# A gated linear attention with an MLP behind it: the input loads get turns of their own, and GpSimd makes the constants

## The chip, the cores and the metric

The kernel runs on one core of a Trainium2 chip. The metric is the time of one execution on the device, in microseconds (us). For the kernel before, the median of three runs is 440.69 us (437.28 to 443.71). The profile below comes from one more execution, which took 438.34 us; the span from its first to its last instruction is 436.6 us. The engines are named as the profile names them: PE (TensorE matmuls), PEld (its weight loads), DVE (VectorE), ACT (ScalarE), POOL (GpSimd), SP (SyncE, which here does nothing but start DMA transfers, in the order of the program). The granted TensorE clock was 1.00 of full speed.

## The reference, cut to what matters

```python
# q, k, v, alpha: (B=4, H=8, S=768, D=48), float32
for t in range(S):
    state = alpha[:, :, t, :, None] * state + einsum('bhd,bhe->bhde', k[:, :, t], v[:, :, t])
    y[:, :, t] = einsum('bhd,bhde->bhe', q[:, :, t], state)
x = y.transpose(0, 2, 1, 3).reshape(B, S, H * D)          # 4 x 768 x 384
xn = (x - mean(x)) / sqrt(var(x) + 1e-6) * g_ln
out = x + maximum(xn @ w_ch1, 0) @ w_ch2                  # 384 -> 1536 -> 384
```

The two weight matrices arrive as 64-bit floats and are rounded to 32 bits on the chip.

## The kernel before, in words

**Tiling.** The sequence is cut into six chunks of 128 tokens. One *step* of attention is one chunk of one batch, so there are 6 x 4 = 24 steps, lettered a to x: a to d are the four batches of chunk 0, e to h those of chunk 1, and so on. A step goes through these stages, each on the line given:

- `la` = Ln(alpha) on ACT (L277); cumulative sums of it as a matmul with the triangle `tri` (`lps`, L283 in chunk 0, L287 in later chunks); Exp of these with both signs on ACT (L290, L291); k and q times those on DVE (`qk`, L293 and L295).
- eight PE transposes with the identity `ident` (`tps`, L320), copied out by ACT and DVE (L325, L327); the scores (`aps`, L336 in chunk 0, L344 later), put under a mask by DVE (`at`, L349 or L354); k times v (`ups`, L370); the state update (L379 on DVE, later L383 on DVE and L385 on POOL) with a `gate` that goes out to DRAM as a row and comes back as columns (two small DMAs, L300 and L360); and the output (`yps`, L396 or L406).
- the layer norm (L413 to L439) and three transposes into `xT` (`xps` on PE, L445, then L448 on DVE or L452 on ACT).

The MLP of chunk 0 multiplies plainly: a *hidden turn* (L475, letters Y for batches 0 and 1, Z for 2 and 3) makes one of 12 column blocks for two batches, and L487 projects back. The chunks after it use a scheme with fewer products (hidden products L764, second products L587) and more additions on DVE and POOL.

**Weights.** They come in 12 pieces of 768 KB (L191). Each is rounded by five DVE instructions (L203 to L213) and one on ACT (L209) before PE may use it. Column blocks 0 and 1 of the hidden layer need piece 0, blocks 2 and 3 piece 1, and so on.

**Order.** Nothing is scheduled at run time. Each stage is a Python generator that records its instructions up to its next `yield`. The string `ORDER` has one letter per `next()`: a letter lets its generator record one more part. So `ORDER` alone fixes the order in which each engine's queue is filled, and SP's queue too. Every engine works through its queue in order and waits on semaphores.

**Loads.** They have no letters in the kernel before. The four loads of alpha for chunk 0 stand ahead of everything. k, q and v of chunk 0 are issued by the attention steps of batches 0 and 2. Alpha, k and q of chunks 1 and 2 are issued together at one fixed place in the steps of batches 1 and 3 of the chunk before (the call `load(c + 1, b // 2, "akq")`), a pair of batches per transfer (384 KB each). From chunk 3 on, `load_one` does the same a batch at a time (192 KB each) into buffers that were claimed once. `v`, and a copy `vx` with its half chunks crossed, are issued behind the output of a step. Alpha, k and q share six buffers (`tag="in"`), so a new load waits for the last read of the tile that lay in its buffer. SP waits in its queue for that, and whatever is queued behind waits too. In the built program every transfer also waits for the one that was issued eight before it, since there are eight completion semaphores.

**Constants.** `tri`, `ident` and a triangle for half chunks lie side by side in one tile `consts` of 128 x 320. The host puts them into the program, and ACT's queue loads them (160 KB) at the start.

Of the kernel before, what the change touches and what calls it, by code (L numbers as in the profile page):

```python
# [9 lines left out]
FP32 = mybir.dt.float32  # L10
# [4 lines left out]
AOP = mybir.AluOpType  # L15
# [7 lines left out]


ORDER = (
    "aaaabbddcccaacbababbaaaadbbbbaaaccdfbbbbcaeeeafcadbbbcecAfedgAccdddeeeeedghffcAc"
    "caabbbdddffffcccfbAgggihbheceeejeeeifaagggggedddjhhchaagdfffBcfiijeejjbbaafkhecc"
    "cffiBjhhjehjjjggYYcciiiBBYYiihddgghhldddChffffhhfYCffYYYddkhiiklCkjhjileegigegjk"
    "jjlCZZZZZZAlDgCFhfgeDZBhYZFZYhhllhhhYlYOiEgjDDFklkEkkilZOgZgggnYmkYYYmEEillllmjj"
    "llZimmnnknkkiYYZZimoZZGiGYYnnnnYYSSHYHSSmGemmmZZZepHZYnFIGnZZOZlIkkkHkomlojJSgJm"  # L30
    "mIJjjKkkkkIQQiSZkLQSjQmmmmmipSniPPPKOKSLLWppooWPWWWhfggnhhfXXiXSSSiXXXPPjjXXPooo"
    "WQiQpQQXpimkkXXOOlnnWmkkmMMnnWmmmlMMMSSSlMMoSMMrrSooWMMMrMMMMMPRqMMMMRnkkMMMoMjr"
    "lRpMMMppMnlnpoooonqqlppppppqqWMMMMqMMMMMMMMMMMMoOolljmMMnnMMMJqsMMOWMpMlMMMqqMRR"
    "RRRMMRMMMMlqsqqrrttqoNNooRRppqqNNppnssMWMRMMqMMMNNNNMMjNsNNsMMMMqMWMMNpNMjMMMMNM"
    "tttNNMMMMurrrrMMMMMrqXqXXXMMMMXXnOntsXXXssoXMsqqMMMMMMMMMMMMMXnMMMRMMMMMMtMMrrtt"
    "qqMMMrrrvMvttuutssssssrttuOMMOOMMMMrvvMMMMmMtpptMMMMMMMpMMMMMtMMRRRRRsRRsttsMrrs"
    "LssmvvmMMMMMrRNNMMpNNppMMMMMRrRonovsosMvMssoMMNNvNNNMvMMtMMuuwMNssRNMMMNNuuuuMMM"
    "MMMrrxMMNMMNqrtNMMMMoMxvvvvoXOwuuuunXXXXXMtttXMMMMMMXXXXuOMMMMtMMMxxxtMMMMMMMMRM"
    "OqOwMMMMwwMMMMMMMMvvtMMMRMMMMMtqMMRMRRRMuMMqqMMMMMwwwwwMMMMxxMMMMMMMxxwwwRxRRNNu"
    "uvwvvxMxxxxwMMRRMMMMvwNNNNNNMuRMMMMNxxxwwwwwMMMMMMwrrNNNMuMwwNMMMMXrXXXXXMMNNNMM"  # L40
    "MMMuMMMMMXXMMMMvMMMwXXxxXMMMMMMMOOvvMMMMMxMuvuMMMRMMMMMMMMMRRRuMMMMMMMxMMMKMMMMM"
    "MMMMMMxxxRRMMMMRMMMMRRxMMMNNNRuwMMMMNRMMMvvuXXXXXXXXXOMMMNNNMMMMVVVVXXVVVNVMVVNN"
    "OMVVVVMMMVVVVRNNVVVMMMMNMVVNVVVVMMNVVVVVVVVVVRRVVVVVRRMMMVMMVVVRRRMMMVVMMVONVVVO"
    "VRMMVRVVVRNNVVMNMNMMMMMRNOMMMMNMMMNONMMMMMVRNNNMMMNNMMMMMMMMMNMNMMNMMMMMMMMM"
)


# [1 line left out]
def kernel(  # L49
# [51 lines left out]
    raw = ctx.enter_context(tc.tile_pool(name="raw", bufs=B // 2))  # L101
# [7 lines left out]

    HS = P // 2  # L110
    halves = [slice(HS * s, HS * s + HS) for s in range(2)]
    r = np.arange(P)
    const_np = np.concatenate([np.triu(np.ones((P, P), np.float32)), np.eye(P, dtype=np.float32),
                               np.tile(np.triu(np.ones((HS, HS), np.float32)), (2, 1))], 1)

    raws = {}

    def load(c, m, names):

        bs = range(2 * m, 2 * m + 2)  # L120
        rows = slice(c * P, (c + 1) * P)
        for n, src in (("a", alpha), ("k", k), ("q", q)):
            if n in names:
                t = raw.tile([P, 2, 2, NP, D], FP32, name=f"r{n}", tag="in", bufs=6)
                step = 1 if n == "a" and c == 0 else 2
                for i in range(0, 2, step):
                    nc.sync.dma_start(
                        t[:, i:i + step].rearrange("t b i p d -> t b (i p d)"),
                        src[bs.start + i:bs.start + i + step, rows].rearrange("b t h d -> t b (h d)"))
                raws.update({(n, c, b): t[:, b - bs.start] for b in bs})  # L130
        if "v" in names:
            vn = raw.tile([P, 2, 2, NP, D], FP32, name="vn", tag="vn")
            nc.sync.dma_start(vn.rearrange("t b i p d -> t b (i p d)"),
                              v[bs.start:bs.stop, rows].rearrange("b t h d -> t b (h d)"))
            vx = None
            if c:


                vx = raw.tile([P, 2, NP, D], FP32, name="vx", tag="vx")
                src = v[bs.start:bs.stop, rows].rearrange(  # L140
                    "b (s t) (i p) d -> s i t b (p d)", s=2, i=2)
                for h in range(2):
                    nc.sync.dma_start(vx[halves[h]].rearrange("t b p d -> t b (p d)"),
                                      src[1 - h, 1 - h])
            for b in bs:
                raws["v", c, b] = vn[:, b - bs.start], vx[:, b - bs.start] if c else None

    lone = {}

    def load_one(n):  # L150

        c, b = divmod(n, B)
        for n, src in (("a", alpha), ("k", k), ("q", q)):
            if n not in lone:
                lone[n] = raw.tile([P, 2, 2, NP, D], FP32, name=f"r{n}", tag="in", bufs=6)
            t = raws[n, c, b] = lone[n][:, b % 2]
            rows = src[b, c * P:(c + 1) * P]
            nc.sync.dma_start(t.rearrange("t i p d -> t (i p d)"),
                              rows.rearrange("t h d -> t (h d)"))
# [5 lines left out]
    for m in range(B // 2):  # L165
        load(0, m, "a")

    w1 = cpool.tile([P, NJ // 2, NF, 2 * P], FP32, name="w1")
    w2 = cpool.tile([P, NJ, DM], FP32, name="w2")
# [79 lines left out]
    def eq_of(c, b):  # L249
        return eqs[b if c < 2 else b % 2]  # L250
# [13 lines left out]
    def attention(c, b):  # L264


        whole, last = c == 0, c + 1 == NCB
        if whole and b % 2 == 0:
            load(0, b // 2, "kq")
            yield  # L270
            load(0, b // 2, "v")
            yield

        qk = qk_of(c, b).rearrange("t n p i c -> t n i p c")[:, :, :, :, :D]
        eq = eq_of(c, b).rearrange("t p i c -> t i p c")[:, :, :, :D]
# [5 lines left out]
        a = las.pop((c, b))  # L281
# [28 lines left out]
        yield  # L310
        at = ats[b % len(ats)]
        if not whole:
# [46 lines left out]
        with nc.allow_non_contiguous_dma(reason="two rows to columns"):  # L359
            nc.sync.dma_start(gate[:, :ne], row[:ne].rearrange("o (p r) -> r o p", p=NP))  # L360
        yield
        vn, vx = raws["v", c, b]
# [29 lines left out]
        for p in range(NP):  # L392
            for i in range(2):
                for s in range(2):
                    if whole:
                        nc.tensor.matmul(yps[0][halves[s], i, p], at[:, p, i, s], vn[:, i, p],  # L396
                                         start=True, stop=True)
                        continue
                    for r in range(2):
                        if r == i:  # L400
                            rs = slice(64 * i, 64 * i + D)
                            of, by = qT[rs, p, s], (now, mid)[s][rs, p]
                        else:
                            of, by = at[halves[r], p, s], (vn[halves[r], i, p] if s == r else
                                                           vx[halves[r], p])
# [436 lines left out]
    turns |= {chr(ord("A") + i): take_weights(i) for i in range(len(pieces))}  # L842
    turns |= {"M": mlp(), "V": hidden_products(NCB - 1), "S": combine_first(), "W": combine_weights(), "R": relus(),
# [34 lines left out]
```

## Time and profile before

| | before |
|---|---|
| median of three runs (lowest, highest) | 440.69 us (437.28, 443.71) |
| the profiled execution | 438.34 us |
| its span | 436.6 us |
| PE busy | 426.7 us, 98% |
| DVE busy | 339.8 us, 78% |
| ACT busy | 201.6 us, 46% |
| POOL busy | 149.7 us, 34% |
| moved by DMA | 45.53 MB, mean 104 GB/s |
| DMA in 0 to 10, 10 to 20, 20 to 30 us | 271, 284, 275 GB/s |

The shares are means over a span whose parts differ. [...] In the last row the DMA engines move between two and three times the mean of the span.

### The profile page before, as it was taken

Reading aid. Unit: us, or ns where it says so; the run is one execution under the profiler, and the core shown is the slowest. Engines: PE = TensorE matmul, PEld = TensorE weight load, DVE = VectorE, ACT = ScalarE, POOL = GpSimd, SP = SyncE. Lnnn points to the kernel's source line nnn. Section 1 sums busy time; section 2 is a strip of 40 time slices with the busy share of each in tenths; the row PEclk is TensorE's granted clock in tenths of the full one; section 3 lists DMA queues with packets and bytes.
Section 4 is the critical chain, followed back from the end, with each engine's and each line's share of the span. In section 5 each row is a group of like instructions: output and inputs, shape, how many; then the busy total and the mean of one; then the engine's idle time right before and its main releaser. Section 6 shows DMA issues by size and latency. Waiting matters only on the chain.

```text
span 436.6 us, 11599 instructions
## 1 busy us (share of the span) xinstructions
PE 426.7 (98%) x4760; PEld 380.9 (87%) x4760; DVE 339.8 (78%) x654; ACT 201.6 (46%) x499; POOL 149.7 (34%) x164
## 2 busy tenths in 40 slices
PE   7988999999999999999999999999999999999996
PEld 5877888876668889999889999889998899999996
DVE  3976989999989788986767758666886589956874
ACT  4687777662325665223277643454505643041100
POOL 1002110111002753051854050872043670756514
PEclk9999999999999999999999999999999999999999
DMA  8988799755035451316214035100014000001201
GB/s 281 289 239 230 202 293 305 186 165 165 2 114 142 98 178 41 108 38 136 67 38 148 18 74 165 1 2 4 20 56 144 2 1 2 0 20 54 72 8 67
DMA packets 54973, 45.53 MB, mean 104 GB/s; under 512 B 26204, under 2 KB 51036, under 8 KB 54920
## 3 DMA queue, kind: packets, MB, share of 16 engines
q1 hardware_dynamic: 54376, 44.63, 34.9%
q8 instruction: 37, 0.61, 0.6%
q10 hardware_dynamic: 544, 0.17, 0.2%
q14 instruction: 16, 0.13, 0.1%
HBM read 35.25 MB, written 9.53 MB: 103 GB/s over the span
## 4 chain that ended last, share of the span: by engine, by line
PE 85%; DVE 5%; DMA 5%; ACT 1%; SPq 0%; issue 0%; DVEq 0%
PE hps L764 30%; PE ops L587 29%; PE ops L487 7%; PE hps L475 4%; PE yps L406 4%; PE tps L320 3%; DMA ws<-in_moe_w_ch_dram 3%; PE aps L344 3%; DMA ra<-in_alpha_dram 2%; PE xps L445 2%; PE ups L370 2%; PE lps L287 1%; DVE w L205 1%; DVE at L354 1%; DVE w L213 0%; PE yps L396 0%
## 5 line engine op out<-in xcount | busy, mean ns | idle before, releaser
L603 POOL TENSOR_TENSOR ob<-ob,u 128x192 f32<-128x192 f32 x40 | 26.9, 683 | 66.8 <-DVE ob L600 56.4
L764 PE MATMUL hps<-sum,w 128*128 128x256 f32 x192 | 47.7, 379 | 0.0
L385 POOL TENSOR_TENSOR mid<-mid,gate 112x192 f32<-112x192 f32 x20 | 10.8, 548 | 98.7 <-DMA gate<-row 48.5
L587 PE MATMUL ops<-w,hT 128*128 128x192 f32 x224 | 40.1, 327 | 0.0
L764 PEld LDWEIGHTS hps<-sum,w 128*128 128x128 f32 x192 | 35.9, 190 | 4.5
L815 ACT ACTIVATE hT<-hT 128x512 f32<-128x512 f32 x48 | 28.3, 625 | 23.7 <-POOL hT L786 15.7
L587 PEld LDWEIGHTS ops<-w,hT 128*128 128x128 f32 x224 | 36.8, 190 | 0.4
L764 PE MATMUL hps<-xT,w 128*128 128x256 f32 x136 | 34.7, 380 | 0.0
L475 PE MATMUL hps<-xT,w 128*128 128x256 f32 x144 | 33.6, 383 | 0.5 <-ACT xn L429 0.5
L487 PE MATMUL ops<-w,hT 128*128 128x384 f32 x96 | 32.0, 488 | 0.0
L475 PEld LDWEIGHTS hps<-xT,w 128*128 128x128 f32 x144 | 26.4, 190 | 4.2 <-ACT xn L429 0.6
L327 ACT COPY qT<-tps 112x512 f32<-112x512 f32 x24 | 13.8, 579 | 35.3 <-PE tps L320 35.2
L597 DVE TENSOR_TENSOR ob<-ops,ob 128x192 f32<-128x192 f32 x50 | 17.3, 352 | 16.4 <-PE ops L587 7.1
L587 PE MATMUL ops<-ws,sum 128*128 128x192 f32 x160 | 28.5, 326 | 0.0
L487 PEld LDWEIGHTS ops<-w,hT 128*128 128x128 f32 x96 | 17.8, 190 | 11.5 <-ACT x L413 0.2
L764 PEld LDWEIGHTS hps<-xT,w 128*128 128x128 f32 x136 | 25.2, 190 | 3.0
L320 PE MATMUL tps<-consts,qk 128*112 128x128 f32 x176 | 24.7, 275 | 2.6 <-DVE qk L295 2.5
L587 PEld LDWEIGHTS ops<-ws,sum 128*128 128x128 f32 x160 | 26.4, 190 | 0.1
L320 PEld LDWEIGHTS tps<-consts,qk 128*112 128x112 f32 x176 | 20.0, 133 | 6.4 <-DVE qk L295 3.4
L587 PE MATMUL ops<-ws,hT 128*128 128x192 f32 x128 | 23.5, 327 | 0.4 <-DVE hT L574 0.4
L344 PE MATMUL aps<-qT,kT 48*64 48x64 f32 x640 | 23.7, 221 | 0.0
L783 POOL TENSOR_TENSOR hT<-hT,u 128x512 f32<-128x512 f32 x8 | 10.3, 1287 | 37.0 <-DVE u L782 37.0
(230 smaller groups left out, 1171.7 us busy)
## 6 DMA issues: line engine op xcount, KB each, us to landing
ws<-in_moe_w_ch_dram SPq DMA_DIRECT2D x12, 768.0 KB
vn<-in_v_dram SPq DMA_DIRECT2D x12, 384.0 KB
kept<-x SPq DMA_DIRECT2D x24, 192.0 KB
ob<-kept SPq DMA_DIRECT2D x24, 192.0 KB
out_dram<-ob SPq DMA_DIRECT2D x19, 192.0 KB
ra<-in_alpha_dram SPq DMA_DIRECT2D x16, 192.0 KB
rk<-in_k_dram SPq DMA_DIRECT2D x6, 384.0 KB
rq<-in_q_dram SPq DMA_DIRECT2D x6, 384.0 KB
```

The lines of the kernel that those rows point to most:

```text
L320: nc.tensor.transpose(tps[:, p], qk_of(c, b)[:, i, p].rearrange("p a b -> p (a b)")[:, :R], ident)
L327: nc.scalar.copy(out=qT, in_=tv)
L344: nc.tensor.matmul(aps[0][halves[1 - i], p, s], kT[rs, p, s], qT[rs, p, s], start=True, stop=True)
L385: nc.gpsimd.tensor_mul(new, new, by)
L406: nc.tensor.matmul(yps[r][halves[s], i, p], of, by, start=True, stop=True)
L475: nc.tensor.matmul(hps, w1[:, j // 2, f, j % 2 * P:][:, :P], xT_of[0][:, f, bs], start=(f == 0), stop=(f == NF - 1))
L487: nc.tensor.matmul(ops_of[b], hT_of[c][:, j, b], w2[:, j], start=(j == 0), stop=(j == NJ - 1))
L587: nc.tensor.matmul(acc, lhs[:, j], rhs[:, j], start=(j == 0), stop=(j == NT - 1))
L597: nc.vector.tensor_add(x, acc, x)
L603: getattr(nc.gpsimd, f"tensor_{op}")(x, x, y)
L764: nc.tensor.matmul(acc[:, i], w, b, start=True, stop=True)
L815: nc.scalar.activation(out=x, in_=x, func=AFT.Relu)
```

## The change

Three things change; the arithmetic on PE, DVE and ACT has the same instructions in the same numbers (2,512 matmul instructions, 636 on DVE).

First, the loads of alpha, k, q and v become four generators with the letters 0 to 3, so that each single transfer has a place of its own in `ORDER`. Chunk 0 is loaded a batch at a time for k and q too, which makes four transfers more (229 on SP against 225). From chunk 3 on, the buffers stay as they were.

Second, `consts` is made by seven GpSimd instructions, and its DMA goes away.

Third, `ORDER` is another string, 1,546 letters for 1,516. It orders all work anew, not only the loads.

```diff
 ORDER = (
-    "aaaabbddcccaacbababbaaaadbbbbaaaccdfbbbbcaeeeafcadbbbcecAfedgAccdddeeeeedghffcAc"
...
+    "00aa00b1cda1a2b22bcc11103abbccdaaa2abbbbdcc2caabbbcffeeedda0bbAabfffaadaeef1dddf"
+    "hfc3dfbghAbddfgaaacbac2dddbhAghcccadbefebhge3ehhh0hggjfggfA3fbhajhBcccgecee2dfff"
...
-    def load(c, m, names):
...
-    def load_one(n):
...
+    def loads(n):
+        src = {"a": alpha, "k": k, "q": q}[n]
+        lone = None
+        for c in range(NCB):
+            for m in range(B // 2):
+                if c < 3:
+                    t = raw.tile([P, 2, 2, NP, D], FP32, name=f"r{n}", tag="in", bufs=6)
+                elif lone is None:
+                    t = lone = raw.tile([P, 2, 2, NP, D], FP32, name=f"r{n}", tag="in", bufs=6)
+                step = 2 if 0 < c < 3 else 1
                 for i in range(0, 2, step):
+                    bs = slice(2 * m + i, 2 * m + i + step)
                     nc.sync.dma_start(
                         t[:, i:i + step].rearrange("t b i p d -> t b (i p d)"),
+                        src[bs, c * P:(c + 1) * P].rearrange("b t h d -> t b (h d)"))
+                    raws.update({(n, c, 2 * m + j): t[:, j] for j in range(i, i + step)})
+                    yield
+
+    def loads_of_v():
+        for c in range(NCB):
+            for m in range(B // 2):
...
+                nc.sync.dma_start(vn.rearrange("t b i p d -> t b (i p d)"),
+                                  v[bs, rows].rearrange("b t h d -> t b (h d)"))
+                raws.update({("v", c, 2 * m + i): vn[:, i] for i in range(2)})
+                yield
+                if c:
...
+                    for h in range(2):
+                        nc.sync.dma_start(vx[halves[h]].rearrange("t b p d -> t b (p d)"),
+                                          src[1 - h, 1 - h])
...
+                    yield
 
     consts = cpool.tile([P, 2 * P + HS], FP32, name="consts")
-    nc.scalar.dma_start(consts, nc.inline_tensor(const_np, name="consts").ap())
...
+    nc.gpsimd.memset(tri, 1.0)
+    nc.gpsimd.affine_select(out=tri, in_=tri, compare_op=AOP.is_ge, fill=0.0, base=0,
+                            pattern=[[1, P]], channel_multiplier=-1)
+    nc.gpsimd.memset(ident, 0.0)
+    nc.gpsimd.affine_select(out=ident, in_=ident, compare_op=AOP.not_equal, fill=1.0, base=0,
+                            pattern=[[-1, P]], channel_multiplier=1)
+    nc.gpsimd.memset(consts[:, 2 * P:], 1.0)
+    for h in halves:
+        part = consts[h, 2 * P:]
+        nc.gpsimd.affine_select(out=part, in_=part, compare_op=AOP.is_ge, fill=0.0, base=0,
+                                pattern=[[1, HS]], channel_multiplier=-1)
...
-        if whole and b % 2 == 0:
-            load(0, b // 2, "kq")
-            yield
-            load(0, b // 2, "v")
-            yield
...
-        n = c * B + b + 2
-        if c < 2 and b % 2:
-            load(c + 1, b // 2, "akq")
-        elif n == 3 * B + 1:
-            load_one(n - 1)
-            load_one(n)
-        elif 3 * B + 1 < n < NCB * B:
-            load_one(n)
-        yield
...
-        if not last and b % 2:
-            load(c + 1, b // 2, "v")
-        yield
...
+    turns |= {"012"[i]: loads("akq"[i]) for i in range(3)} | {"3": loads_of_v()}
```

In the new order the first transfers on SP are alpha of the four batches, then k and q of batch 0 and 1, each batch by itself. The first weight piece stands in both orders behind the same 5.12 MB of transfers (itself counted). The second stands behind 8.49 MB instead of 10.46 MB, the third behind 10.47 MB instead of 12.25 MB, the fourth behind 11.25 MB instead of 14.03 MB. The second pair of v of chunk 0 stands behind 5.92 MB instead of 3.15 MB, alpha for batches 2 and 3 of chunk 1 behind 4.34 MB instead of 5.52 MB, and alpha for the first pair of chunk 2 behind 7.50 MB in both. The last 45 matmul instructions and what follows them are the same products in the same order.

On POOL the new queue begins with two memsets of 128 x 128, then the setting that POOL makes before its first arithmetic instruction (a MODIFY_POOL_CONFIG in the trace; before, it stands at the first L385), the selects for `tri` and `ident`, a memset, the memset of the first `at`, the selects for the half triangles, and the memset of the second `at`.

More of the change, by code (lines that the diff above doesn't have):

```diff
@@ new lines @@
+    "fJPekKKhhehhQnooSSSeehLfOikkkggieggnnL22SiQjgL33nnjpgq00WWPP3SXXrXSjkXpPkniSSWnX"
+    "nnoWOSXnnWkPOkknXQiQmQpmSSSippnkmllnnnplpl3ppmnXMPXXWmMMMWMMjMMMOOOSMXMMmmmMMMMM"
+    "QMMmooMMMMoMMMroppqoooooRkRnppp1o13WqpMq2qkkMMMooMMMjMMMM3WM3MMWMMMnn0tMMMpRRMMR"
+    "MMMMRMqqqMMM1MssqWqqqRrr1pRpoqpppMLMM0RMNNssNNWMMMMRRRMMNNNNNjj2lollOOMMrMNMM2MN"
+    "NuqqooMM3WMMsl2MMMM2rlmmrMMMjMNNNNMsMMMMMMMMMssqrrMMXjXXsMMMuXX1rrtsqqXXXXqttqqq"
+    "tMMMMMXX0MMMMMMMMMMM0wMMMMqqMMvtMMttstMMMMr0rrvstpusttttRRsvMMuMMM11sMrMpMMMM2pM"
@@ L45 @@
+    "MVVVVVVVVVNNNNNNNVVVVVVVVMMXMVVVMMMMMNNMNNNNVVVMMVVVVVVMVVOMMMMVVVVVVVVVVVMRMMVV"
+    "NNVVNVMMMVVMVRVRRVVVVVKRMMOVVVVMOMRRRRMMMNRMMRRMNNMMMNNNMMMMOMMMMMNNMMMNNNNMMMMJ"
+    "OMMMNMMNMNMMMNMMMMMMMMMMMM"
 )
@@ L111 @@
     halves = [slice(HS * s, HS * s + HS) for s in range(2)]
-    r = np.arange(P)
-    const_np = np.concatenate([np.triu(np.ones((P, P), np.float32)), np.eye(P, dtype=np.float32),
-                               np.tile(np.triu(np.ones((HS, HS), np.float32)), (2, 1))], 1)
     raws = {}
-    def load(c, m, names):
[L120 to L125, printed above, removed]
+    def loads(n):
[8 more added lines that the diff above has]
+                step = 2 if 0 < c < 3 else 1
@@ L126, in load @@
                 for i in range(0, 2, step):
+                    bs = slice(2 * m + i, 2 * m + i + step)
                     nc.sync.dma_start(
                         t[:, i:i + step].rearrange("t b i p d -> t b (i p d)"),
[L129 to L146, printed above, removed]
@@ L148 @@
-    lone = {}
-    def load_one(n):
[L152 to L159, printed above, removed]
+                        src[bs, c * P:(c + 1) * P].rearrange("b t h d -> t b (h d)"))
@@ new lines, in loads @@
+                    raws.update({(n, c, 2 * m + j): t[:, j] for j in range(i, i + step)})
[3 more added lines that the diff above has]
+            for m in range(B // 2):
+                bs, rows = slice(2 * m, 2 * m + 2), slice(c * P, (c + 1) * P)
+                vn = raw.tile([P, 2, 2, NP, D], FP32, name="vn", tag="vn")
+                nc.sync.dma_start(vn.rearrange("t b i p d -> t b (i p d)"),
[3 more added lines that the diff above has]
+                if c:
+                    vx = raw.tile([P, 2, NP, D], FP32, name="vx", tag="vx")
+                    src = v[bs, rows].rearrange("b (s t) (i p) d -> s i t b (p d)", s=2, i=2)
+                    for h in range(2):
+                        nc.sync.dma_start(vx[halves[h]].rearrange("t b p d -> t b (p d)"),
+                                          src[1 - h, 1 - h])
+                    raws.update({("x", c, 2 * m + i): vx[:, i] for i in range(2)})
+                    yield
@@ L361, in attention @@
         yield
-        vn, vx = raws["v", c, b]
+        vn = raws["v", c, b]
         heads = [slice(0, 64), slice(64, R)]
@@ L404, in attention @@
                             of, by = at[halves[r], p, s], (vn[halves[r], i, p] if s == r else
[L405 removed]
+                                                           raws["x", c, b][halves[r], p])
                         nc.tensor.matmul(yps[r][halves[s], i, p], of, by, start=True, stop=True)
```

29 lines of the change are left out of this document (9 added, 20 removed).

## The prediction

> **What bounds the kernel now.** I read the page first (busy shares, then the slices over time), next what PE waited for, then the rows of the start and the DMA rates by stretch, and last the chain.
>
> ```profile
> span 436.6 us, 11599 instructions
> ...
> PE 426.7 (98%) x4760; PEld 380.9 (87%) x4760; DVE 339.8 (78%) x654; ACT 201.6 (46%) x499; POOL 149.7 (34%) x164
> ...
> PE   7988999999999999999999999999999999999996
> ...
> DMA  8988799755035451316214035100014000001201
> ```
>
> PE is the bound. It has room only in the first six or so slices (10.9 us each) and in the last. The DMA engines are busy in just those first slices and mostly idle later. So there are two stages: a front of about 65 us with PE short of work, and a rest in which PE never stands.
>
> ```profile
> PE tps L320 <- DVE qk L295: 2.5, 2, 1.4
> PE lps L287 <- ACT la L277: 1.9, 2, 1.3
> ```
>
> These two (in total, times, longest) are most of PE's waits. Both have a load behind them:
>
> ```profile
> 8.32 0.56 DVE L293 TENSOR_TENSOR qk<-rk,lps 128x384 f32<-128x384 f32 x1 [5.65 <-DMA rk<-in_k_dram]
> 9.24 0.56 DVE L295 TENSOR_TENSOR qk<-rq,eq 128x384 f32<-128x384 f32 x1 [0.36 <-DMA rq<-in_q_dram]
> ...
> 9.86 2.02 PE L320 MATMUL tps<-consts,qk 128*112 128x128 f32 x16 [1.18 <-DVE qk L295]
> ...
> 29.45 0.52 ACT L277 ACTIVATE la<-ra 128x384 f32<-128x384 f32 x1 [1.62 <-DMA ra<-in_alpha_dram]
> ```
>
> PE's first transposes (9.86) wait for DVE, and DVE for k and q; at 29.45 alpha of chunk 2 is late. The DMA engines were full meanwhile (columns after the busy times: clock, DMA share, GB/s):
>
> ```profile
> 0.00:10.00 10.00, 7.78 (x25) 5.68 (x26) 3.14 (x14) 4.81 (x9) 2.04 (x6) 1.00 0.84 271
> 10.00:20.00 10.00, 9.47 (x162) 7.94 (x162) 8.86 (x18) 5.39 (x13) 0.00 (x0) 1.00 0.94 284
> 20.00:30.00 10.00, 8.69 (x177) 7.45 (x175) 9.60 (x17) 8.21 (x22) 0.95 (x1) 1.00 0.92 275
> 30.00:40.00 10.00, 9.78 (x250) 9.03 (x251) 6.76 (x17) 9.44 (x29) 1.91 (x3) 1.00 0.74 181
> ```
>
> The chain says the same, and shows SP at 34.88 held up by a buffer, with a weight piece behind it:
>
> ```profile
> 24.80 4.62 DMA ra<-in_alpha_dram
> ...
> 34.88 0.37 SPq L127
> 35.30 1.25 SPq L360
> 36.60 6.36 DMA ws<-in_moe_w_ch_dram
> ...
> 405.98 27.32 PE ops L587 x168
> ```
>
> **PE's lateness.** Busy time hides the losses of the front, so I count otherwise: the work ordered ahead of an instruction on PE, at the pace of the trace, taken from its start. The paces are from starts to starts, long stops left out: eight transposes 0.93 us, scores of a step of chunk 0 1.0, of a later step with its `lps` 1.05, `yps` 1.0, `ups` 0.3 (0.6 later), `xps` 0.34, a hidden turn 1.34, the warm-up 3.6, `lps` of chunk 0 2.6 for all four. The first hidden turn (L475) has 30.1 us ahead and starts at 39.09: 9.0 late. The fifth has 37.1 ahead and starts at 48.31: 11.2 late. The last has 78.5 ahead and starts at 89.7: still 11.2. After that only 0.4 us is lost (244.7), and 3.3 us pass behind the last matmul. So 11.2 us of the 436.6 are lost in the front. What the change does to that number is what it does to the time.
>
> **The change, part by part.**
>
> *Work.* Same matmuls, DVE and ACT instructions: 0. Four transfers more cost SP 4 x 0.4 = 1.6 us of issuing (L127, 0.37 to 0.43 each). SP idles for tens of us later, and in the front the DMA backlog hides it; without that cover it is 1.6 us at most. The tail is the same products in the same order: 3.3 us stay.
>
> *Order of the loads.* To fit the late alpha: 7.50 MB stand up to it on SP, 0.16 of `consts` beside them; at 277 GB/s (mean of the first three stretches) 27.7 us, and it was used at 29.45, so 1.8 more. With that fit each load gives a lateness: the arrival less the PE work ahead of its user.
> - Before: alpha of chunk 2 arrives at 29.45, 21.6 ahead: 7.9 late. The second weight piece landed at 42.98 and was rounded by 48.17 (5.2 us of DVE), 37.1 ahead: 11.1 late. That is the 11.2.
> - After, alpha of chunk 2: 27.1 + 1.8 = 28.9, now with 26.4 ahead: 2.5.
> - After, second pair of v in chunk 0 (moved back): 5.92 MB, 21.4 + 1.8 = 23.2, its `ups` has 18.8 ahead: 4.4. This is the latest load.
> - After, second weight piece: 8.49 MB, 30.6 + 1.8 + 5.2 = 37.6, 37.1 ahead: 0.5. Third: 37.8 + 7.0 = 44.8, 44.3 ahead: 0.5.
> With 4.4 in the place of 11.1, what is late next is DVE.
>
> *DVE in the front.* From the first mask copy (L349, at 13.05) to the second `xT` (L448, done at 38.9) it had 21.7 us of work in 25.9. In the new order 18.3 us stand between the same two. A start near 13.0 gives 31.3 plus waits of 1.5 (the gates and v as above) to 4.2 (as before): 32.8 to 35.5 for the first hidden turn, with 29.1 ahead. Lateness 3.7 to 6.4.
>
> *Constants on POOL.* No select and no setting of POOL with nothing else to wait for is in the trace. A select costs between 0.1 (memset 128x1) and 1.3 us (POOL on 128x512, L783, 1,287 ns); I take 0.5, the nearest in size (L385, 112x192, 548 ns). For the setting there is this row (durations, first and last start):
>
> ```profile
> L385 POOLq MODIFY_POOL_CONFIG  x2: 9/9/9, 28.1 to 28.2; - x2
> ```
>
> POOL's next event is at 33.12, 5.0 us on, but the profile lays this wait to a gate's DMA. So the setting costs 0 to 5.0; I take 5.0, since nothing shows that POOL could have begun earlier. Two memsets from 0.73 (0.17 each, as DVE's L227): `tri` is ready at 1.1 + 5.0 + 0.5 = 6.6, where before PE had it by 4.5. Then `lps` 0.65, the two Exp 0.8, k and q on DVE 1.0: first transposes at 9.1 to 9.3, not 9.86, as k and q of batch 0 alone stand behind 1.38 MB, not 1.57 + 0.16 (0.35 / 0.277 = 1.3 us sooner, 7.9). At a cost of 0, k and q decide, and transposes begin at 8.6 or so. Both are under the old time; `ident` (7.1) and the `at` memsets (8.2 and 10.1) are ready before their users (9.2 and 12). If this cover went, each us of POOL would be a us of PE's start.
> [...]
>
> *The middle.* Behind 100 us of PE work, loads in the new order have 5.4 us or more between the point of PE's work where SP can issue them and the use; before, the shortest were 6.5 and 7.2 and no wait came of them. I cost this at 0, hidden behind PE; if one load of 192 KB met a full queue it would be 1 to 2 us.
>
> *Sum.* Lateness by loads 4.4, by DVE 3.7 to 6.4; the two mix, so 6.0, against 11.2: 5.2 us gained. 438.34 - 5.2 = 433.1 for an execution like the profiled one. The runs' median lies 2.35 above it, so I forecast **435.5** as a median. The runs spread over 6.4 us, and 2% (8.8 us) is about what a measurement of this kernel can tell from no change.
>
> **Rivals.**
> 1. *The gain is made in the front and lost again in the middle.* For: the new order is another one throughout, and its tightest round trips from PE over ACT or DVE and back have only 0.4 to 0.6 us to spare at some six places. Against: the order before has such places too (0.5 us), with a single wait of 0.4 us after 68 us. Five such waits of 1 us each take it all: 440.5.
> 2. *SP runs dry (slower).* Loads of 192 KB fill the eight places with 1.6 MB at most, 5.7 us at 277 GB/s; with pairs 2.4 to 3.1 MB. SP in the new order stands at `row` and `gate` transfers at about 9 to 14 us, with a weight piece and the second v behind them. Each us of empty DMA engines puts that v a us later. From 11.2 - 4.4 = 6.8 us of emptiness on, the kernel is slower than before. For it: in 30 to 40 us the rate fell to 181 GB/s while SP was held up for 2.3 us. Against: by 10.4 us 3.9 MB can be issued, work for 14 us. At twice that emptiness, 13.6: 440.69 + 6.8 = 447.5.
> [...]
> 4. *Much better than this:* v and DVE are no bound, and only the start remains, 3.0 us (9.2 less 6.2 ahead): 8.2 gained, 432.5.
>
> **How the numbers follow.** Forecast 0.55, rival 1 0.20, rival 2 0.10, rival 3 0.07, rival 4 0.08. Range 430 to 442: the low end is rival 4 with the runs' scatter, the high end rival 1 with it; rival 2 is left out. Faster by over 2% (under 431.9) needs rival 4 and a good run: 0.10. Slower by over 2% (over 449.5) is the worse part of rival 2 and unseen waits: 0.08. Within 2%: 0.82.
>
> **What would show it.** First transposes at 8.6 to 9.4 (POOL's part; over 10 speaks for rival 3), the setting of POOL at about 1.1 and its first select at most 5 us later; the first hidden turn at 33 to 36, not 39.09; no wait of DVE's L203 for the second piece; PE without waits of over 0.5 us from 50 us on; the last matmul 3.3 us ahead of the end. A DMA rate under 240 GB/s in 10 to 30 us, or PE waits in the middle that add up to 3 us, would make me wrong.

## The result, and the profile after

The changed kernel takes **436.76 us** as a median (433.0 to 440.07, 20 runs), the kernel before 439.41 us in the same series (436.96 to 443.71, 20 runs). The ratio is 0.9937 with a 95% interval of 0.991 to 0.9965: faster by 0.6%, a small gain that is really there. The profiled execution took 435.69 us with a span of 433.9, against 438.34 and 436.6 before. So some 2.7 us came, where the forecast counted 5.2 for an execution like that one.

The page of the changed kernel, in the order in which the page of the kernel before was read (span, busy time by engine, then the busy tenths of PE and of the DMA engines in 40 slices of 10.8 us):

```profile
span 433.9 us, 11625 instructions
...
PE 425.5 (98%) x4760; PEld 380.3 (88%) x4760; DVE 336.1 (77%) x654; ACT 202.6 (47%) x499; POOL 149.8 (35%) x171
...
PE   8999998999999999999999999999999999999996
...
DMA  8877869675435614314233024022012100001201
```

PE is the bound as before. The front of PE is a little fuller, but its seventh slice (65 to 76 us) has an 8 where the kernel before had a 9. What PE waited for (total, times, longest), by the view of waits:

```profile
PE hps L458 <- DVE ws L211: 1.6, 1, 1.6
...
PE tps L306 <- DVE qk L290: 0.9, 2, 0.8
PE lps L282 <- ACT qT L313: 0.8, 1, 0.8
```

The two large entries of before (2.5 at the transposes, 1.9 at `lps`) are down to 0.9 and 0.8. A new one of 1.6 us stands in front of a hidden turn. The chain of waits in the first 75 us shows both (start, duration, what):

```profile
18.85 5.80 DMA vn<-in_v_dram
24.69 0.61 PE ups L356 x13
...
26.53 6.32 DMA ra<-in_alpha_dram
32.87 0.52 ACT la L272
...
33.92 0.75 PE lps L282 x3
...
37.04 2.79 PE hps L458 x12
...
69.64 0.82 issue
70.46 4.58 PE hps L458 x20
```

The second pair of `v` is issued at 18.85 and used at 24.69; alpha of chunk 2 is issued at 26.53 and used at 32.87; the hidden turns begin some 4 us of PE's program behind it. By the count of the prediction (start on PE less the PE work ordered ahead):

| point | before | forecast after | after |
|---|---|---|---|
| first transposes | 9.86 us | 9.1 to 9.3 | 9.31 |
| `ups` with the second `v` pair, late by | | 4.4 | 5.9 |
| `lps` of chunk 2 with its alpha, late by | 8.4 | 2.5 | 7.5 |
| first hidden turn, start / late by | 39.09 / 9.0 | 32.8 to 35.5 / 6.0 | 36.97 / 7.9 |
| at 100 us, late by | 11.1 | 6.0 | 9.1 |
| last PE instruction starts | 432.95 | | 430.35 |

The forecast counted the alpha from its arrival, not from the start of `lps`; so counted, it is 7.9 before and 6.5 after (used at 32.87, 26.4 ahead) where 2.5 was forecast. Of the 11.1 us, 2.0 are gone by 100 us, and the later part loses 0.6 less than before (2.6 in all at the last PE instruction).

### The profile page after: what moved, and what is told of

Read it like the earlier page. It is cut to its first block, busy times and chain, and to the rows that moved or that the text cites. A ratio compares the mean times of both kernels' runs of the same rounds, so it can differ in the third digit from the quotient of the medians.

```text
span 433.9 us, 11625 instructions
## 1 busy us (share of the span) xinstructions
PE 425.5 (98%) x4760; PEld 380.3 (88%) x4760; DVE 336.1 (77%) x654; ACT 202.6 (47%) x499; POOL 149.8 (35%) x171
## 4 chain that ended last, share of the span: by engine, by line
PE 92%; DMA 4%; SPq 1%; issue 1%; DVE 1%; ACT 1%; DVEq 0%
PE hps L747 30%; PE ops L570 30%; PE ops L470 7%; PE hps L458 7%; PE yps L392 5%; PE aps L330 4%; PE tps L306 3%; PE ups L356 2%; PE xps L428 2%; DMA ra<-in_alpha_dram 1%; DMA vn<-in_v_dram 1%; DMA rk<-in_k_dram 1%; SPq L128 1%; PE lps L282 1%; PE aps L322 0%
## 5 line engine op out<-in xcount | busy, mean ns | idle before, releaser
L586 POOL TENSOR_TENSOR ob<-ob,u 128x192 f32<-128x192 f32 x40 | 25.7, 653 | 65.4 <-DVE ob L583 51.7
L371 POOL TENSOR_TENSOR mid<-mid,gate 112x192 f32<-112x192 f32 x20 | 13.3, 671 | 81.3 <-DVE mid L369 54.8
L470 PEld LDWEIGHTS ops<-w,hT 128*128 128x128 f32 x96 | 17.7, 190 | 10.8
L570 PEld LDWEIGHTS ops<-ws,sum 128*128 128x128 f32 x160 | 26.4, 190 | 0.2
L435 ACT ACTIVATE xT<-xps,small 128x128 f32<-128x128 f32 x48 | 13.8, 372 | 20.4 <-PE xps L428 20.4
```

The lines of the kernel that those rows point to most:

```text
L371: nc.gpsimd.tensor_mul(new, new, by)
L435: nc.scalar.mul(xT_of[c][:, f, b], xps[:, f], g_col[:, f:f + 1])
L470: nc.tensor.matmul(ops_of[b], hT_of[c][:, j, b], w2[:, j], start=(j == 0), stop=(j == NJ - 1))
L570: nc.tensor.matmul(acc, lhs[:, j], rhs[:, j], start=(j == 0), stop=(j == NT - 1))
L586: getattr(nc.gpsimd, f"tensor_{op}")(x, x, y)
```

## Where the front still waits: SP's order

The DMA engines by stretch (PE, PEld, DVE, ACT and POOL busy, granted clock, DMA share, GB/s), in the changed kernel:

```profile
10.00:20.00 10.00, 9.84 (x168) 8.28 (x167) 8.66 (x18) 6.16 (x15) 0.00 (x0) 1.00 0.84 269
20.00:30.00 10.00, 9.71 (x194) 8.47 (x193) 8.97 (x18) 9.01 (x26) 2.29 (x2) 1.00 0.73 229
30.00:40.00 10.00, 9.13 (x225) 7.98 (x224) 7.86 (x15) 7.45 (x22) 1.57 (x3) 1.00 0.82 218
```

From 20 to 30 us they moved 229 GB/s where they moved 275 before. They were not full: SP stood. The waits of SP in the first 75 us (total, times, longest):

```profile
SPq L295 <- ACT lps L286: 11.7, 5, 5.8
...
SPq L408 <- ACT few L411: 3.4, 1, 3.4
SPq L408 <- ACT x L399: 2.5, 1, 2.5
```

SP issues in order. The transfer of `row` (L295) waits for ACT's Exp, that of `kept` (L408) for `x`, and every load behind them in ORDER waits too. The forecast had used bytes alone for the arrivals. Three runs ask what this costs; each moves one or both of two letters of ORDER.

**Both loads earlier.**

```diff
-a0bbAabfffaadaeef1dddfhfc3dfbgh...befebhge3ehhh0hggj
+a0bbA3abfffaadaeef10dddfhfcdfbgh...befebhge3ehhhhggj
```

> The changed kernel with two letters moved: the second pair of v of chunk 0 is issued ahead of the two row transfers for which SP stood from 15.3 to 17.3 us, and alpha of chunk 2 behind k of chunk 1, ahead of the kept and gate transfers for which it stood from 19.3 to 21.9 and later. Theory (SP stands in front of these loads, and they set the lateness of the front): v is there by about 22 in the place of 24.64, alpha of chunk 2 by about 27 in the place of 32.87, PE's stops at 24.7 and 33.9 go, the first hidden turn starts at 34.8 to 35.5 in the place of 36.97, and the time falls by 1.4 to 2.2 us, to 434.6 to 435.4. Rival (DVE and ACT need that long in the front, and the loads only hide it): both loads land earlier, yet the first hidden turn stays at 36.5 to 37 and the time at 436.3 to 437.

Measured: **433.84 us** (433.02 to 434.23, 5 runs), ratio to the kernel before 0.9873 (0.9851 to 0.9896), so 0.6% faster than the changed kernel, the lowest median of all, and below the 434.6 to 435.4 expected. Alpha of chunk 2 is used at 31.63, `v` at 24.37 with no wait, the first hidden turn starts at 35.80, 6.7 us late in the place of 7.9:

```profile
24.37 0.61 PE L356 MATMUL ups<-vn,more 128*64 128x48 f32 x15
...
31.63 0.54 ACT L272 ACTIVATE la<-ra 128x384 f32<-128x384 f32 x1
...
35.80 2.86 PE L458 MATMUL hps<-xT,w 128*128 128x256 f32 x12
```

The front gave 1.2 us, a little less than expected. PE's waits:

```profile
PE tps L306 <- DVE qk L290: 1.7, 2, 1.6
...
PE xps L428 <- DVE xn L418: 0.4, 1, 0.4
PE yps L392 <- DMA vx<-in_v_dram: 0.4, 1, 0.4
```

There is no `hps` among them: the stop at 70 us is not there, which nobody had expected of this run. That is the other half of its gain; the section on the stop deals with it.

**Only `v` earlier**, the first of the two letters.

> The changed kernel with only the second pair of v of chunk 0 moved ahead (the first of the two letters of the run with loads earlier, which gained 1.2 us of lateness at the first hidden turn). Theory: v was used 0.9 us late at 24.7, but alpha of chunk 2, 1.3 us late at 33.9, comes after it and was issued behind v in the same row of SP; v alone lets the stop at 24.7 go and moves the first hidden turn by 0 to 0.5 us: 436.4 to 436.9 us as a median, since the stop at 69 us stays in some executions. Rival: v is the load that sets the front, as the forecast had it: first hidden turn at 35.8, time 435 to 435.6.

Measured: 436.22 us, ratio 0.9943 (0.9912 to 0.9975), as the changed kernel. `ups` starts at 23.92, but the first hidden turn at 37.13. So `v`, which the forecast had as the latest load, holds nothing by itself.

**Only alpha earlier**, the second letter.

> The changed kernel with only alpha of chunk 2 moved ahead (the second of the two letters). Theory: this load, used at 32.87 where the forecast had 28.9, is what holds the first hidden turn: it starts at 35.8 to 36.2 in the place of 36.97, time 435.2 to 436.2 where the stop at 69 us stays, 434 where it goes. Rival (v sets it): first hidden turn at 36.7 to 37, time as the changed kernel's.

Measured: 435.39 us, ratio 0.9909 (0.9876 to 0.9943). The first hidden turn starts at 36.62, a gain of 0.35, less than expected and not clear of the scatter (in three other traces with the changed kernel's front it starts at 36.57 to 37.01): `v` is now used at 25.36, with a wait of 1.5 us, and that takes the place of the alpha. The two loads set the front together; to move one alone exposes the other.

## The lists against loads in the attention turns

The changed order of the work was run with loads of chunks 0 to 2 in the attention turns, about where the kernel before has them (k, q and v of chunk 0 in one go).

```diff
+        if whole and b % 2 == 0:
+            load(0, b // 2, "kqv")
...
         nc.sync.dma_start(row[:ne], eq_of(c, b)[ends].rearrange("o p i c -> o (p i c)"))
+        if c < 2 and b % 2:
+            load(c + 1, b // 2, "akq")
...
+        if c < 2 and b % 2:
+            load(c + 1, b // 2, "v")
```

> The changed kernel's order of work on PE, DVE, ACT and POOL, but alpha, k, q and v of chunks 0 to 2 are loaded where the kernel before loads them: with the attention turns, k, q and v of a pair in one go, pairs of 384 KB (from chunk 3 on as changed). It tells what carries the gain, the order of the work or the lists of loads. Theory (the lists: each load late enough to let a nearer one pass): the first weight pieces and v stand behind more bytes again, first transposes at 9.9, the first hidden turn at 38 to 40, time 438.5 to 440.5. Rival (the new order of the work gives it, loads come early enough in any case): 436.3 to 437.2, first hidden turn at 36.5 to 37.5.

Measured: **446.7 us** (443.71 to 449.36), ratio 1.0158 (1.0108 to 1.0208), 7 us slower than the kernel before and some 10 slower than the changed one: more than expected. With its loads there, the new order of the work loses; the old order was not run with lists. The first hidden turn starts at 46.16, and the chain points at another reason than "bytes ahead of the weights". PE's waits, and three pieces of the chain of waits:

```profile
PE yps L430 <- POOL mid L409: 3.7, 1, 3.7
PE tps L344 <- DVE qk L326: 3.4, 3, 1.5
PE xps L468 <- DVE xn L458: 2.5, 1, 2.5
```

```profile
19.12 3.21 DMA gate<-row
...
28.00 4.84 DMA gate<-row
...
37.51 6.08 DMA gate<-row
```

A gate is a transfer of 2 to 4 KB, out to DRAM as `row` and back as `gate`. Issued behind three or four loads of 384 KB at once, it lands 3.2, 4.8 and 6.1 us later, and POOL, DVE and PE stand for the state that it scales; PE's wait of 3.7 us follows the longest of the three. Between 40 and 50 us PE is busy for 6.3 us of 10, and the mean granted clock in that stretch is 0.69 where the four stretches of 10 us ahead of it have 1.00:

```profile
40.00:50.00 10.00, 6.33 (x103) 5.39 (x95) 5.27 (x12) 3.19 (x12) 2.61 (x4) 0.69 0.46 128
```

## The constants

On POOL in the changed kernel (start, duration):

```profile
0.80 0.20 POOL L156 MEMSET consts<- 128x128 f32 x1 [0.29 <-POOLq L844]
0.94 0.21 POOL L159 MEMSET consts<- 128x128 f32 x1
1.18 0.29 POOL L157 TENSOR_SCALAR_AFFINE_SELECT consts<-consts 128x128 f32<-128x128 f32 x1
1.43 0.29 POOL L160 TENSOR_SCALAR_AFFINE_SELECT consts<-consts 128x128 f32<-128x128 f32 x1
```

The settings (durations in ns, first and last start):

```profile
L157 POOLq MODIFY_POOL_CONFIG  x2: 12/12/12, 1.1 to 1.1; - x2
```

The two settings of POOL start at 1.09 and 1.12 us, the first select at 1.18. The setting costs 0.06 us, not the 5.0 taken in the forecast. A select of 128x128 takes 0.29 us, where 0.5 was taken.

**Constants by ACT's transfer again**, all else as changed.

```diff
-    nc.gpsimd.memset(tri, 1.0)
-    nc.gpsimd.affine_select(out=tri, ...
...
+    nc.scalar.dma_start(consts, nc.inline_tensor(const_np, name="consts").ap())
```

> The changed kernel with one part undone: the constants come by ACT's transfer of 0.16 MB again, as before; the lists and the order of the loads stay. Theory: the start waits for ACT's four Ln (the fourth alpha was used at 6.66 us), not for the constants (ready by 1.5 us on POOL), so the part is worth only the bytes that stand before the alphas and k: 0.16 MB at 270 GB/s, 0.6 us at most. First transposes at 9.3 to 9.9 us, time 436.7 to 437.4. Rival: the constants made the gain (POOL ready early lets everything start), and the lists none: first transposes at 9.9 and the time at the kernel before's 439.4.

Measured: 436.65 us, ratio 0.9939 (0.9911 to 0.9967), first transposes at 9.37. The part is worth nothing that can be measured.

**Constants by POOL in the kernel before.**

> The kernel before with one part of the change alone: constants by POOL, old order, old loads. Theory: 0 to 0.6 us gained (the 0.16 MB that leave the front, of 11.2 us of lateness): 438.8 to 439.4; first transposes at 9.3 to 9.9, since k and q of batch 0 still stand behind 1.57 MB. Rival: the constants made the gain: 436.8. The setting of POOL should again cost about 0.06 us between it and the first select, whatever the program.

Measured: 439.07 us, ratio 0.9992 (0.9974 to 1.0009). The same answer from the other side. The select again starts at 1.18 us. The first transposes came at 10.55 in this execution, later than expected: DVE's first product waited for k until 8.94 us, so constants don't set the start in that order either.

By the timeline of ACT, the start in the changed kernel stands behind four Ln in a row that ACT takes ahead of the first Exp:

```profile
6.66 0.52 ACT L272 ACTIVATE la<-ra 128x384 f32<-128x384 f32 x1 [1.15 <-DMA ra<-in_alpha_dram]
7.09 0.47 ACT L285 ACTIVATE eq<-lps 128x384 f32<-128x384 f32 x1
7.46 0.48 ACT L286 ACTIVATE lps<-lps 128x384 f32<-128x384 f32 x1
```

The first Exp starts behind the fourth Ln, which waits for its load. One run changes that, on top of the run with both loads earlier.

```diff
-00aa00b1cda1a2b22bcc11103
+00aa12ba00b1a2bcd2cc11103
```

Alpha's two buffers of chunk 0 are taken ahead of the lists there, so that the buffers turn over as before.

> The kernel of the run with two loads earlier, and the start in another order: alpha, k and q of the first two steps are loaded ahead of alpha of the other two, and ACT takes a step's Exp ahead of the next step's Ln. It tests what sets the first transposes (9.27 there). Theory (ACT's fourth Ln waits for a load at 6.66, and the first Exp stands behind it; k and q are next): q of batch 0 is the fourth load in the place of the seventh, lands by about 6.7, first transposes at 7.3 to 8.0. Whether that reaches the end: if the whole front is one chain, the lateness of the first hidden turn falls from 6.7 by as much, and the time to 432.3 to 433.0; if v and alpha of later steps and DVE set it, the first hidden turn stays at 35.5 to 36 and the time at 433.5 to 434.

Measured: 434.2 us (432.67 to 438.24, 6 runs), ratio 0.9892 (0.9845 to 0.9939): no better than without it (433.84; four of the six runs took 432.7 to 434.3, two 437.9 and 438.2). DVE's first product did come earlier, at 7.12 in the place of 7.97, but the first transposes came at 9.76 in the place of 9.27. PE takes `lps` of the third and fourth step ahead of the first transposes, and their Ln now came last (PE waited 1.4 us for it). The theory looked at ACT alone and missed PE's own order. The first hidden turn started at 37.05 in this execution, so the 1.2 us of the two loads were lost again. Whether an earlier start is worth something is open: in two other kernels with the changed kernel's front, transposes began at 8.85 and 8.87 and the first hidden turn at 36.96 and 37.01, no earlier than with 9.31; but in the last run below, which has both loads earlier too, 8.67 and 34.91 stand against 9.27 and 35.80.

## The stop at 70 us: PE without instructions

The profile lays this stop to DVE's rounding of a weight piece. But the hidden turn behind it reads another piece, rounded long before, and the one DVE result that it waits for (`x`, L402, for its PSUM bank) was done at 68.0 us, 2.4 us before it started.

**Without most of the rounding of the sixth piece.**

```diff
            op0=AOP.bitwise_and, op1=AOP.bitwise_or)
+        if i == 5:
+            yield
+            yield
+            return
```

> The changed kernel without most of the rounding of the sixth weight piece: of its five DVE instructions only the first is left, and ACT's is out too, so that piece's weights are wrong values. It tells what stopped PE for 1.56 us at 70.46. Theory A (the profile's word for it: DVE, busy with this piece from 65.2 to 70.6, was late): the stop is gone, PE goes on at 68.9, time down by about 1.5 us to 435.2. Theory B (PE lacked its own instructions: a packet of 16 KB of them came from 67.97 to 68.86, after 455 instructions of PE where 190 to 300 lie between most packets): a stop of 1 to 1.6 us stays at the same hidden turn though DVE is 3.5 us lighter, and the time within 0.5 us of 436.8.

Measured: 437.91 us, ratio 0.996 (0.9937 to 0.9983), over the 436.3 to 437.3 of theory B. This piece's L211, named by the profile, is not there any more, yet the stop is there, longer than theory B had it, and another line gets the blame:

```profile
PE hps L462 <- DVE w L209: 2.6, 1, 2.6
```

Theory A falls. What was common was the place: if all of PE's rows in the trace (matmuls, weight loads, and the few semaphore rows among them) are numbered in order of their start, the stop comes behind row 2,240 in both kernels. So the program was shifted.

**Eight small matmuls more in the warm-up.**

```diff
         nc.tensor.matmul(idle[:, :P], zero, zero, start=True, stop=True)
+    for _ in range(8):
+        nc.tensor.matmul(idle[:, :P // 4], zero, zero[:, :P // 4], start=True, stop=True)
```

> The changed kernel with eight small matmuls (128x32) more behind the eight of the warm-up, some 32 rows of PE in the trace, about 1 us, beside loads that are waited for anyhow. If PE's stop at 70.46 is one for its own instructions, it belongs to a place in the program as counted in instructions, not to a matmul: it then comes 32 rows sooner in the work, inside the small matmuls ahead of the hidden turn at 67.33, and the turns behind it run on; still 1 to 2 us long. If a tile or a semaphore makes it, it stays between the same two hidden turns. Time 436.5 to 438 in both cases.

Measured: 439.41 us, ratio 0.9966 (0.9933 to 1.0), slower than expected with a wide spread (435.97 to 444.39); the profiled execution took 436.17. The timeline of PE:

```profile
66.69 0.52 PE L358 MATMUL ups<-vn,qk 64*64 64x48 f32 x21
68.72 0.38 PE L358 MATMUL ups<-vn,qk 64*48 64x48 f32 x10 [1.51 <-issue]
69.03 3.29 PE L460 MATMUL hps<-xT,w 128*128 128x256 f32 x14
```

The stop moved 32 rows forward in the work, into the middle of one tile's small matmuls, where no tile and no semaphore can end, and the hidden turns behind it run on. It is again behind row 2,240. The same kernel stops behind row 1,472 for 0.8 us and behind 8,128 for 1.2; many of the others, the changed kernel too (0.63 us at 299.7), stop behind 8,128. The distances are 768 and 5,888 rows, 3 and 23 times 256. The page lists what comes in such portions:

```profile
q8 instruction: 37, 0.61, 0.6%
```

Those are 37 packets of 16,384 bytes. That each holds 256 rows of PE's program is the author's estimate; the count agrees with it: 37 x 256 is 9,472, and PE has some 9,600 rows. And some packets start right behind such places: those of 46.16, 72.49 and 102.90 us in the changed kernel start 5, 19 and 11 rows behind rows 1,472, 2,240 and 3,008. That fits packets that are asked for one portion ahead of their use. In time, from the rows and the DMA records of the traces (the 1,985th row is 256 ahead of the 2,241st):

| kernel | row 1,985 | packet from, to | row 2,241 | stop | packet's end to row 2,241 |
|---|---|---|---|---|---|
| before | 58.85 | 59.90, 60.79 | 64.86 | none | |
| both loads earlier | 64.51 | 65.18, 66.29 | 67.60 | none | 1.3 |
| constants by DMA | 66.04 | 68.03, 68.92 | 70.50 | 1.36 | 1.58 |
| changed | 65.42 | 67.97, 68.86 | 70.45 | 1.94 | 1.59 |
| sixth rounding out | 65.31 | 68.52, 69.71 | 71.42 | 3.01 | 1.71 |
| eight matmuls more | 65.12 | 66.25, 67.23 | 68.72 | 1.73 | 1.49 |

(The stop here is from start to start, so it has one matmul in it.) Wherever PE stopped at this row, it went on 1.4 to 1.7 us behind the end of the packet (1.3 in the last run below), and in the kernels with the same 256 rows the later the packet, the longer the stop. The changed order lets PE run these rows in 3.1 us, since 243 of them are small matmuls of the attention and their weight loads in one go; in the order before they took 6.0 us. So a packet that starts 2.5 us behind row 1,985 and takes 0.9 comes too late.

Two runs tried to get rid of it.

**Three loads moved behind the packet.**

```diff
-iiiZ22YYZZZkFZZZ0H3FZ3ill
+iiiZYYZZZkFZZZH3FZ3220ill
```

> The changed kernel with three letters moved: two loads of q (384 and 192 KB, issued at 66.0 and 66.7 us) and one of alpha (192 KB, 67.5) come some 3 us of issuing later, behind the v pair issued at 68.0 to 69.3 and the hidden turns next to it. It tests why PE's packet of instructions came late before the stop at 70.46. In the runs so far the packet started 0.8, 2.1, 2.7 and 3.3 us behind PE's 1,980th row of the trace (the run with the loads earlier, the one with constants by DMA, the changed kernel, the one without the sixth rounding), and the stop was 0, 1.0, 1.56 and 2.6 us. Theory (the packet queues behind data on the DMA engines): with 0.77 MB out of its way it starts under 1.2 us behind that row, the stop is under 0.5 us, time 435.0 to 435.9. Rival (the packet's lateness has to do with PE's own pace alone, a burst of small matmuls): packet and stop as they were, 436.3 to 437.

Measured: 438.54 us, ratio 0.9975 (0.995 to 1.0001), slower than expected. The packet started 2.0 us behind row 1,985 and the stop was 1.36 us: a miss, since the run with the constants by DMA had the same with these loads in place. Another wait of 1.5 us had come at 84 us. Why the packet starts 0.7 us behind that row in one kernel and 3.2 in another is open; data in the DMA engines at that moment are not shown to be the reason.

**One hidden turn ahead of the small matmuls.**

```diff
-ZZZZjF1EhgEGhhhFggiiiZ22YYZZZk
+ZZZZYYjF1EhgEGhhhFggiiiZ22ZZZk
```

> The changed kernel with one hidden turn (its product and its Relu, 12 rows of PE, 1.3 us) moved from behind to ahead of the small matmuls of the attention at 65 to 67 us; no load is moved. Theory (PE stops at its 2,241st row of the trace when the packet that starts with it has not come; five runs stopped there and went on 1.5 to 1.7 us behind the packet's end): from the 1,980th to the 2,241st row PE now has 1.3 us more to do, so the gap of 1.94 us in the rows shrinks to about 0.6 or goes, and the time falls by 0.8 to 1.4 us, to 435.4 to 436.0. Rival (the packet is asked for when PE gets near its end, and comes later by as much): gap as before, 436.5 to 437.

Measured: 437.97 us, ratio 0.9976 (0.9949 to 1.0003). The edit had the wrong sign. The turn went ahead of row 1,985, not between the two rows, and pushed a turn that had been inside the 256 out at their end. The rows then passed in 1.9 us in the place of 3.1, and the gap grew from 1.94 to 3.54 (1.2 us of it from the rows; the packet also started later, 3.0 us behind row 1,985 in the place of 2.5):

```profile
PE hps L458 <- issue: 3.3, 1, 3.3
```

The theory's other numbers hold: the stop is behind row 2,240, the packet ends at 69.75 and PE goes on at 71.23, 1.5 us later. The rival, a packet that is asked for near the end of the rows, would have kept the gap.

In this execution the stop cost more than its own length. PE went on at 71.23, and behind that the granted clock was 0.50 for 3.4 us, in which PE did 10 matmuls; behind a stop of 3.0 us in the next run it was 1.00, and PE did 16. The two stretches (columns as above):

```profile
71.60:75.00 3.40, 3.40 (x10) 2.69 (x9) 3.37 (x7) 0.38 (x1) 1.24 (x2) 0.50 1.00 316
...
69.00:72.40 3.40, 3.36 (x16) 2.97 (x17) 3.33 (x6) 0.77 (x2) 0.81 (x1) 1.00 1.01 300
```

Half the clock for 3.4 us is up to 1.7 us of PE's work (an estimate: 0.5 x 3.4), and it makes a mean of 0.996 over the execution. The profiled execution of the run with the start in another order had the same behind a stop of 2.5 us; the one without most of the rounding kept 1.00 behind 3.0 us. The means of the other executions point the same way: 6 of the changed kernel's 20 had 0.996 and took 438.2 to 440.1 us, the other 14 had 0.999 or more and took 433.0 to 437.7; in this run 9 of 12 had 0.995 or 0.996, with both loads earlier none of 5. So the medians in this section differ in part by how many executions lost some clock. That they lost it behind this stop is shown for the two profiled ones alone; the kernel before, which has no such stop, had a mean under 0.998 in 16 of 82.

**Both loads earlier, and that turn.**

> The run with both loads earlier (433.84) and the hidden turn of the first of these four moved ahead as well: the best of the parts. That run had no stop at the 2,241st row, by a margin of some 0.1 us in its profile, so the turn can add little: 433.4 to 434.0, with no execution above 434.5. If moving the turn delays the attention behind it, a wait of DVE or PE of 0.5 to 1.5 us shows at 67 to 86 us, and the time is 434.3 to 435.3.

Measured: 437.54 us (434.63 to 438.68), ratio 0.996 (0.9931 to 0.9989), against 433.84 without the turn, and not the best of the parts as expected. One letter pair that changes no work and no load costs 3.7 us as a median, part of it by the clock: 9 of the 12 executions had a mean of 0.995 or 0.996, and the other three took 434.63 to 436.32. The profiled execution, the fastest, has the stop at row 2,241 with 3.0 us. The 256 rows passed in 1.85 us, and the packet came from 66.69 to 67.75, so it started 2.5 us behind row 1,985 where it started 0.7 behind it without the turn. With 0.7, these rows would have stopped for about 1.2 us (an estimate: 0.7 + 1.1 + 1.3 - 1.85); the rest is the later packet. So how fast the rows pass is shown to be one part of the stop, by this run and the one before it; how late the packet starts is the other, and why it does stays open.

## Why the prediction was right, and where it was off

The forecast (435.5, within 2% of before) stands, 1.3 us under the median. For an execution like the profiled one it said 433.1 and 435.69 came: of the 5.2 us that it counted, 2.7 came. That the median agrees better is partly luck: the forecast added 2.35 us because the median of three runs lay that much above the profiled execution; over 20 runs it lay 1.07 above (439.41), and with that the same sum gives 434.2. By its steps:

- *Work* and *tail*: right. The same matmuls; from the start of the last PE instruction to the end it is 3.6 us in both traces.
- *Constants*: the transposes came at 9.31 where 9.1 to 9.3 was said, but not for its reason. `tri` was ready at 1.5 us, not 6.6; the setting, taken at 5.0 us, measured 0.06. ACT's fourth Ln stood in the same place by chance. The undoing of this part moved nothing.
- *Order of the loads*: the direction was right and the term mis-sized. Alpha of chunk 2 was to arrive at 28.9, 2.5 late, and was used at 32.87, 6.5 late; the second `v` was to arrive at 23.2, 4.4 late, and was used at 24.69, 5.9 late. The working divided bytes by a rate and so took SP for always ahead. SP stood at `row` and `kept`, which the text had only as a rival. What was undone by two letters is 1.2 us at the first hidden turn.
- *Which load is the latest*: wrong. The forecast named `v`; by these numbers it is alpha, and at the first hidden turn `v` alone earlier gave nothing, alpha alone 0.35 at most, both 1.2.
- *DVE in the front*: the size was right and its effect not. The second `xT` was done at 33.5, within the 32.8 to 35.5 given, but the first hidden turn stands behind `lps` of chunk 2 in PE's order and came at 36.97.
- *Second and third weight piece*: the sign came true, since DVE's L203 didn't wait for the second, but not the numbers. The second was to be rounded by 37.6 and was by 44.06, the third by 44.8 and was by 51.22; by the forecast's count that is 7.0 and 6.9 late in the place of 0.5. DVE came to them late (it began the second at 38.06 with no wait for it). PE didn't wait only because it was later still: its fifth hidden turn, the first to need the second piece, started at 45.18. The end of that rounding:

```profile
43.10 0.96 DVE L213 SCALAR_TENSOR_TENSOR w<-w,ws 128x768 f32<-128x768 f32 x1
```

- *Nothing lost behind the front*: wrong by 1.7 us at 69 us, ahead of the part that the forecast calls the middle, and by 0.3 at 300 us in it. At 100 us the forecast is 3.1 us off (9.1 late, not 6.0): 1.9 from the front (7.9 at the first hidden turn), the 1.7 of the stop, and 0.5 won back. The later part then loses 0.6 less than before, which leaves the miss of some 2.5. "PE without waits of over 0.5 us from 50 us on" was the sign, and it failed.

Of the rivals, 1 (lost again in the middle) came true by two fifths of its size (2.0 of 5 us), by a mechanism that it didn't have. 2 (SP runs dry) was at work from 20 us on, at 1.2 us, far from its 6.8; its sign, under 240 GB/s from 10 to 30 us, shows in the second half of that stretch alone (269, then 229). 3 (a late start by POOL's setting) fell: the setting measured 0.06 us, and the transposes came at 9.31, not over 10. 4 (only the start remains) fell too.

## What to carry to other kernels

When arrivals are worked out, walk through the issuing engine's queue with its waits first, and divide bytes by the rate only where that queue is ahead; here small transfers that waited (`row` for 11.7 us in five waits, `kept` for 3.4 and 2.5) held the loads behind them, and a small round trip behind bulk loads took 3.2 to 6.1 us. Count the instructions of an engine as well as its time: where PE went through 256 rows, most of them small matmuls, in 3.1 us, the packet behind them came late by the account above (a stop of 1.94 us), and the profile blamed DVE, though the one DVE result that PE waited for was there 2.4 us before PE went on. Make a stop move before believing a releaser: a few dummy instructions ahead tell a tile's wait from a place in the program.

## What the runs showed that was not expected

37 packets of 16 KB, of the kind "instruction", arrive during the run, and PE stopped behind rows 1,472, 2,240 and 8,128 (256 apart, times 3 and 23); at the second of these places it went on 1.3 to 1.7 us behind the packet's end, and the rows stood 1.4 to 3.5 us apart. Behind two of these stops (2.5 and 3.5 us) the granted clock was 0.50 for 3.4 us, behind two others (3.0 us) it was not. The setting of POOL ahead of a select cost 0.06 us. A transfer of 2 KB behind bulk loads took 4.8 us to land, one of 4 KB 6.1. In the slowest kernel the mean granted clock fell to 0.69 in the one stretch of the front in which PE was busy for 63%.
